# Attention and GEGLU on one core: the softmax sums of batches 3 to 6 move ahead of the next batch's scores, the products with v behind them

## The chip, the cores and the metric

The kernel runs on one core of a Trainium2 chip. Its time is the device time of one execution in microseconds (us); what is compared is the median of several executions. A profile is one execution recorded by the hardware. Engines: PE is TensorE (matmuls), DVE VectorE, ACT ScalarE, POOL GpSimd, SP SyncE (it only issues DMAs and semaphore work here). [...]

## The reference: what is computed

Windowed attention with a linear bias over 8 batches of 8 heads, 576 positions and head size 64, then a gated feed-forward block over all 8 x 576 = 4608 tokens:

```
scores = q @ k.T / 8 + slope[h] * -(i - j),  only for 0 <= i - j < 128
attn   = softmax(scores) @ v                       # per batch and head
x      = attn as [4608, 512]                       # 8 heads x 64 side by side
out    = (gelu(x @ w_gate) * (x @ w_val)) @ w_out  # 512 -> 1536 -> 512
```

All inputs and the output are float32; the kernel works in bfloat16 with float32 sums.

## The kernel before, in words

**Two pipelines on one TensorE.** Attention goes by batch (576 tokens), the feed-forward block by group g of 512 tokens, g = 0 to 8. A group has two parts. The *gate loop* is `gate_val(g, f)` for f = 0 to 11 (L608): eight matmuls of 128x512 each (L625, four with `wg` and four with `wv`, over the four 128-row slices c of `xT`), a gelu by ScalarE (L632), and a product by VectorE into the hidden tile `hT` (L633). The *steps* of the group, `steps(g)` (L906), write out the order of the rest by hand: an integer n stands for n sixteenths of the output product (`out_part`, L650; 4 is one quarter, 12 matmuls on L662, which ends with a copy of the bank to `osb` and a store on SP's queue), and names stand for attention work of batch b = g + 2.

**Attention of one batch.** q and k are loaded by POOL's queue (`load_qk`, L116), transposed by TensorE (`transposes`, L173, matmuls on L178) and copied to `qT`, `kT`. `scores2(b, c0)` (L260) makes the scores of four heads, half a batch: matmuls on L291 into six PSUM banks, six exponentials by ScalarE (L222), four masks by VectorE (L225), which leave the weights in `P`. Some of these matmuls share a bank between two halves of the array; for them `relay` (L201) puts an empty instruction on SP's queue, which waits for the first half's last matmul and lets the second half go. `add` (L371) is VectorE's preparation of the sums, into tile `T`. `sums4` (L419) makes the sums of the softmax with 32 small matmuls (L430) and inverts them with two VectorE reciprocals (L435) into a tile `r` that holds them in a compact form. To have them beside the products, they take a way through DRAM: `gather` (L439) writes them to `rd` in two small DMAs, `spread_dma` (L447) reads `rd` back twice, once for each half of the partitions, and copies each inverse to 64 partitions of tile `rb` (two DMAs of 576 KB). Both are on ACT's queue, and the spread waits for the gather to have landed. `values(b)` (L540) multiplies `P` with v (`products`, L457, matmuls on L494, six banks, with relays of the same kind) and scales the result by `rb` into `xT` (L558, VectorE: four slices of 512 columns, two small ones).

**Order around the change**, for the steps of g = 2 to 5 with b = g + 2: quarter 1; products of batch b - 1; quarter 2; scores of half 0 of batch b and their `add`; quarter 3; scores of half 1 and their `add`; quarter 4. In the gate loop of the next group follow: sums of the batch just scored at f 3 (f 4 in group 2), gather at f 5 (6), spread at f 7 (8), transposes of the batch after it at f 6 and 8, and at f 9 POOL's loads: q and k of batch g + 3 (ten DMAs), v of batch g + 2 (five). A one-element copy into `mark` holds POOL back until the hidden tile of that f is written.

**What the feed-forward block waits for.** Group g + 1 reads 512 tokens of `xT`, beginning at 512 (g + 1); for g + 1 up to 6 these include the first tokens of batch g + 1, which is batch b - 1 of the steps of group g. `xT` is a ring of 3072 tokens, so batch 5 is scaled in two pieces for each slice.

**Buffers.** The 8 PSUM banks are handed out in turn. `P`, `qT`, `kT`, q, k and v have two buffers (even and odd batches), `T`, `r` and `rb` one, `osb` three.

Of the kernel before, what the change touches and what calls it, by code (L numbers as in the profile page):

```python
# [8 lines left out]
BF16 = mybir.dt.bfloat16  # L9
# [23 lines left out]
def kernel(  # L33
# [10 lines left out]
    nc = tc.nc  # L44
    B, H, S, D = q.shape
# [22 lines left out]
    def bank():  # L68
        return psum.tile([128, 512], FP32, name="ps")
# [23 lines left out]
    mark = consts.tile([1, 2], BF16, name="mark")  # L93
# [22 lines left out]
    def load_qk(b):  # L116
        load(qs[b % 2], q, b)
        load(ks[b % 2], k, b)

    def load_v(b, js=range(5)):  # L120
        load(vb[b % 2], v, b, js, 64)
# [79 lines left out]
    def relay(mm, engine=nc.sync):  # L201
        by = engine.nop()
        depends(by, mm)
        return by
# [52 lines left out]

    def scores2(b, c0):  # L260
        pairs = (c0, c0 + 1)
        own, shared = {}, {}
        own[c0, 1] = bank()
        for c in pairs:
            shared[c] = bank()
        for key in ((c0, 0), (c0 + 1, 1), (c0 + 1, 0)):
            own[key] = bank()
        turns = ([(c, True) for c in pairs] + [(c, False) for c in pairs],
                 [(c, False) for c in pairs] + [(c, True) for c in pairs])
        todo, left = [], {}  # L270
        for i, turn in enumerate(turns):
            at = 0
            for c, both in turn:
                if both and i:
                    at = max(at, left[c] + HANDOVER)
                for x in (0, 1):
                    t = at
                    for m, q0, w, col in parts_of(x, both):
                        todo.append((t, i, c, both, x, m, q0, w, col))
                        t += w  # L280
                at = t
                left[c] = at
            if not i:
                left = {c: 256 * (n + 1) for n, c in enumerate(pairs)}
        todo.sort(key=lambda t: t[0])
        count, by = {c: 0 for c in pairs}, {}
        total = sum(len(parts_of(x, True)) for x in (0, 1))
        for _, i, c, both, x, m, q0, w, col in todo:
            half = slice(64 * i, 64 * i + 64)
            ps, col = (shared[c], col + 256 * i) if both else (own[c, i], col)  # L290
            mm = nc.tensor.matmul(  # L291
                out=ps[64 * x:64 * x + 64, col:col + w], lhsT=keys(b, c, m)[half, :],
                rhs=qT[b % 2][half, c, q0:q0 + w], start=True, stop=True)
            if both and i == 0:
                count[c] += 1
                if count[c] == total:
                    by[c] = relay(mm)
            if both and i and c in by:
                depends(mm, by.pop(c))

        def whole(c, i):
            exp(prob(b)[:, c, i, 64:576], own[c, i])

        def ends(c):
            exp(prob(b)[:, c, :, 576:832], shared[c][:, 0:512].rearrange("p (i x) -> p i x", i=2))

        def masks_(c, s):
            mask(prob(b)[:, c, :, 64 + 384 * s:448 + 384 * s], decay(s, c))

        c, d = pairs  # L310
        whole(c, 1)
        whole(c, 0)
        masks_(c, 0)
        ends(c)
        masks_(c, 1)
        ends(d)
        whole(d, 1)
        whole(d, 0)
        masks_(d, 0)
        masks_(d, 1)  # L320
# [50 lines left out]
    def add(b, c0, copy=None, what=(0, 1)):  # L371
        hs = slice(2 * c0, 2 * c0 + 4)
        P = Ps[b % 2].rearrange("p h (n y) -> p h n y", y=64)[:, hs]
        to = T.rearrange("p h (n y) -> p h n y", y=64)[:, hs]
        if 0 in what:
            for x in (0, 1):
                half = slice(64 * x, 64 * x + 64)
                nc.vector.tensor_tensor(  # L378
                    out=to[half, :, x:x + 7:2], in0=P[half, :, 0:10:3], in1=P[half, :, 1:11:3],
                    op=ALU.add)  # L380
            nc.vector.tensor_copy(out=to[0:64, :, 8], in_=P[0:64, :, 12])
            nc.vector.tensor_tensor(
                out=to[64:128, :, 8], in0=P[64:128, :, 11], in1=P[64:128, :, 12], op=ALU.add)
        if 1 in what:
            for x in (0, 1):
                half, n = slice(64 * x, 64 * x + 64), 4 - x
                (copy or nc.vector.tensor_copy)(
                    out=to[half, :, x + 1:x + 2 * n:2], in_=P[half, :, 2:3 * n:3])

    sumrow, recip = {}, {}  # L390
# [45 lines left out]

    flat = {}

    def gather(b):  # L439
        flat[b] = d_pool.tile([H, S], FP32, name="rd")  # L440
        for s in (0, 1):
            lo, w = shape(b, s)
            nc.scalar.dma_start(
                out=flat[b][:, lo:lo + 2 * w].rearrange("h (x t) -> x h t", x=2),
                in_=sumrow[b][0:128:8, lo:lo + w])

    def spread_dma(b):  # L447
        for i in (0, 1):
            nc.scalar.dma_start(
                out=recip[b][64 * i:64 * i + 64, :, :],  # L450
                in_=flat[b][i:H:2, :].unsqueeze(0).to_broadcast((64, 4, S)))

# [153 lines left out]
    hid = {}  # L606
# [34 lines left out]
    acc = {}  # L641


    by_dve = {0: (0,), 1: (0, 1)}

# [69 lines left out]
    for h in (0, 2, 4, 6):  # L717
        for w, src in ((0, q), (1, k)):
            (nc.scalar if w and h == 0 else nc.sync).dma_start(  # L719
                out=raw[w][h // 4].rearrange("p (h x) -> p h x", h=4)[:, h % 4:h % 4 + 2, :],  # L720
                in_=src[0][h:h + 2, 0:384, :].rearrange("h (p r) d -> p h (r d)", r=3))
# [115 lines left out]
    for do in inverse_a:  # L837
        do[1]()
    dve(out=pairs1.rearrange("p x (h d) -> p h x d", d=64),
        in_=vb[1].rearrange("p j x -> p (j x)")[:, 0:1536].rearrange(  # L840
            "p (h x d) -> p h x d", h=H, x=3))
# [46 lines left out]
    for n in range(4):  # L888
        nc.gpsimd.dma_start(
            out=wo[:, 3 * n:3 * n + 3, :],  # L890
            in_=moe_w_out[384 * n:384 * n + 384, :].rearrange("(c p) f -> p c f", p=128))
# [14 lines left out]
    def steps(g):  # L906
        b = g + 2
        if g in todo:
            return todo[g]
        if b > B:  # L910
            return [16] if g < NG - 1 else [12, ("last", g)]
        if b == B:
            return [4, ("pv", b - 1), 12]
        return [("table",), 4, ("pv", b - 1), 4, ("s2", b, 0), ("add", b, 0), 4, ("s2", b, 2),
                ("add", b, 2), 4]


    def exp_table():
        nc.scalar.preload_act_table_set("natural_log_exp_and_others")

    RUN = {"s": scores, "s2": scores2, "add": add, "sum4": sums4, "gather": gather, "spread": spread_dma, "pv": values, "pv+": values_and_sums,
           "masks": flush, "table": exp_table, "transposes": transposes, "last": out_last, "scale": lambda: scales.pop()(), "o": out_half}

    for g in range(NG):
        for f in range(9 if g == 0 else 0, NF):
            gate_val(g, f)
            if g == 1 and f in (5, 7):
                transposes(2, f - 5)
                transposes(2, f - 4)
            if g == 1 and f == 11:  # L930
                transposes(3, 0)
                transposes(3, 1)
                nc.gpsimd.tensor_copy(out=mark, in_=hid[g][0:1, f, 0:2])
                load_qk(4)
                load_v(3)
            if 2 <= g < B - 2 and f in (6, 8):
                transposes(g + 2, f - 6)
                transposes(g + 2, f - 5)
            if g == 2 and f == 2:
                add(3, 2, act, (1,))  # L940
            if g == 0 and f == 10:
                masks_of_last_blocks(0, 8)
            if g == 0 and f == 9:
                for c in range(4):
                    for w in (0, 1):
                        transpose(1, w, c, (act, dve)[w])
            if 2 <= g < B - 1:
                if f == (4 if g == 2 else 3):
                    sums4(g + 1)
                if f == (6 if g == 2 else 5):  # L950
                    gather(g + 1)
                if f == (8 if g == 2 else 7):
                    spread_dma(g + 1)
                if f == 9 and g + 2 < B:

                    nc.gpsimd.tensor_copy(out=mark, in_=hid[g][0:1, f, 0:2])  # L956
                    if g + 3 < B:
                        load_qk(g + 3)
                    load_v(g + 2)
        if g == 0:  # L960
            nc.gpsimd.memset(Ps[0][:, :, 0:64], 0.0)
        for item in steps(g):
            if isinstance(item, int):
                out_part(g, item)
            else:
                RUN[item[0]](*item[1:])
        store()
        if g == 0:
            load_qk(3)
            load_v(2)  # L970
# [30 lines left out]
```

## Time and profile before

| | |
|---|---|
| median of 3 executions | 361.46 us (360.63 to 361.49) |
| the profiled execution | 361.49 us; its span, first to last instruction, 359.7 us |
| granted TensorE clock | 1.000 |
| PE busy | 349.9 us (97% of the span) |
| DVE, ACT, POOL busy | 203.4, 184.4, 105.6 us |
| gate matmuls, L625 | 920, 52% of the chain that ended last |
| output matmuls, L662 | 24% of that chain |
| transposes L178, products L494, scores L291, sums L430 | 6%, 5%, 2%, 1% of that chain |
| one round of the steady part | 39.1 us (gate loop of group 3 from 182.61 to 207.74, its steps to 221.78) |

The chain that ended last is followed back from the last instruction: at each step to what released it, or to the instruction before it on its engine. Busy time of matmuls is modelled, since they overlap in the array; the durations in the chain are from start to start. Times in the timeline are microseconds from the start of the span.

### The profile page before, as it was taken

To read this page: it belongs to the slowest core of one execution; us is meant where nothing else is said; L and a number is where in the kernel's file an instruction comes from. 1 tells how busy PE (TensorE), PEld (TensorE's weight loads), DVE (VectorE), ACT (ScalarE), POOL (GpSimd) and SP (SyncE) were. 2 spreads that over 40 slices of the span, in tenths; PEclk is the share of its full clock that TensorE was granted. 3 is DMA by queue.
4 is the path that set the end of the run, shared out by engine and by line. 5 is a ranking of instruction groups with operands and counts; after the bars stand their busy time and mean duration, and the time that the engine had idled before them with its cause. 6 is when DMAs were issued, how large, how long until landed. Compare 5 with 4: busy or idle time off the path is not lost.

```text
span 359.7 us, 8537 instructions
## 1 busy us (share of the span) xinstructions
PE 349.9 (97%) x3508; PEld 184.7 (51%) x3556; DVE 203.4 (57%) x382; ACT 184.4 (51%) x340; POOL 105.6 (29%) x139
## 2 busy tenths in 40 slices
PE   8999999999999999999999999999999999999996
PEld 6667556555654555454545554455544544444444
DVE  7887865445789546944596458844694413302420
ACT  7964786447696437544473439253753123313322
POOL 6965689406700086004900192004000000000000
PEclk9999999999999999999999999999999999999999
DMA  8999999908950099219990599049203320011002
GB/s 210 171 197 191 200 187 187 124 2 52 162 107 2 5 194 189 64 23 135 170 122 5 131 138 181 3 104 105 81 31 69 95 89 2 0 58 60 0 28 90
DMA packets 118043, 35.65 MB, mean 99 GB/s; under 512 B 101716, under 2 KB 110964, under 8 KB 118004
## 3 DMA queue, kind: packets, MB, share of 16 engines
q0 software_dynamic: 107456, 18.10, 65.2%
q1 hardware_dynamic: 7232, 10.75, 8.5%
q10 hardware_dynamic: 3316, 6.25, 7.9%
q8 instruction: 28, 0.46, 0.5%
q14 instruction: 11, 0.09, 0.1%
HBM read 43.65 MB, written 9.53 MB: 148 GB/s over the span
## 4 chain that ended last, share of the span: by engine, by line
PE 94%; DMA 1%; issue 1%; DVE 1%; ACT 1%; SPq 0%; DVEq 0%
PE ps L625 52%; PE ps L662 24%; PE ps L178 6%; PE ps L494 5%; PE ps L291 2%; PE ps L682 2%; PE ps L209 1%; DMA qs<-in_q_dram 1%; PE ps L430 1%; PE ps L698 1%; PE ps L154 1%; ACT P L222 0%; SPq L719 0%; DVE xT L530 0%; DVE qT L162 0%
## 5 line engine op out<-in xcount | busy, mean ns | idle before, releaser
L633 DVE TENSOR_TENSOR hT<-ps,gelu 128x512 bf16<-128x512 f32 (+3 forms) x117 | 73.8, 646 | 97.6 <-PE ps L625 91.3
L632 ACT ACTIVATE gelu<-ps 128x512 bf16<-128x512 f32 (+3 forms) x117 | 65.1, 564 | 98.5 <-PE ps L625 96.2
L625 PE MATMUL ps<-xT,wg 128*128 128x512 bf16 (+4 forms) x460 | 112.1, 361 | 0.8
L625 PE MATMUL ps<-xT,wv 128*128 128x512 bf16 (+4 forms) x460 | 111.2, 361 | 0.4
L662 PE MATMUL ps<-wo,hT 128*128 128x512 bf16 x374 | 87.6, 380 | 2.1 <-issue 1.4
L625 PEld LDWEIGHTS <-wv 128*128 128x128 bf16 x472 | 45.0, 98 | 48.7
L625 PEld LDWEIGHTS <-wg 128*128 128x128 bf16 x472 | 43.5, 98 | 45.8
L662 PEld LDWEIGHTS <-hT 128*128 128x128 bf16 x396 | 37.0, 98 | 43.3
L222 ACT ACTIVATE P<-ps 128x512 bf16<-128x512 f32 (+1 forms) x108 | 51.3, 583 | 3.9 <-PE ps L209 3.6
L225 DVE TENSOR_TENSOR P<-P,emask 128x768 bf16<-128x768 bf16 x60 | 31.2, 556 | 19.5 <-ACT P L222 17.7
L667 ACT COPY osb<-ps 128x512 f32<-128x512 f32 x27 | 15.9, 588 | 51.3 <-PE ps L662 51.3
L112 POOL DMA_DIRECT2D vb<-in_v_dram x40 | 34.0, 902 | 2.9 <-DMA wo<-in_moe_w_out_dram 1.0
L956 POOL COPY mark<-hT 1x2 bf16<-1x2 bf16 x4 | 0.7, 174 | 108.4 <-DVE hT L633 108.4
L112 POOL DMA_DIRECT2D qs<-in_q_dram x30 | 25.5, 870 | 4.9 <-DMA wo<-in_moe_w_out_dram 2.7
L112 POOL DMA_DIRECT2D ks<-in_k_dram x30 | 25.4, 893 | 0.3 <-PE ps L625 0.3
L181 ACT COPY qT<-ps 128x576 bf16<-128x576 bf16 x22 | 14.0, 638 | 9.8 <-PE ps L178 9.8
L494 PE MATMUL ps<-P,vb 64*64 64x192 bf16 (+2 forms) x752 | 17.7, 221 | 0.6 <-issue 0.4
L558 DVE TENSOR_TENSOR xT<-ps,rb 128x512 bf16<-128x512 f32 (+3 forms) x34 | 14.7, 502 | 4.6 <-PE ps L494 4.6
L494 PEld LDWEIGHTS <-vb 64*64 64x64 bf16 x752 | 14.7, 107 | 4.0 <-issue 3.0
L181 DVE COPY kT<-ps 128x576 bf16<-128x576 bf16 x24 | 11.0, 457 | 5.7 <-PE ps L178 5.1
L378 DVE TENSOR_TENSOR T<-P 64x1024 bf16<-64x1024 bf16 x20 | 13.7, 686 | 0.6
L178 PE MATMUL ps<-ident,ks 128*128 128x128 bf16 (+1 forms) x120 | 12.7, 218 | 0.0
(95 smaller groups left out, 238.0 us busy)
## 6 DMA issues: line engine op xcount, KB each, us to landing
out_dram<-osb SPq DMA_DIRECT2D x35, 256.0 KB, 3.1
rb<-rd ACTq DMA_DIRECT2D x10, 576.0 KB, 6.4
vb<-in_v_dram POOLq DMA_DIRECT2D x32, 128.0 KB, 6.3
qs<-in_q_dram POOLq DMA_DIRECT2D x24, 128.0 KB, 4.5
ks<-in_k_dram POOLq DMA_DIRECT2D x24, 128.0 KB, 6.1
wo<-in_moe_w_out_dram POOLq DMA_DIRECT2D x4, 384.0 KB, 12.3
wg<-in_moe_w_gate_dram POOLq DMA_DIRECT2D x5, 256.0 KB, 8.4
wv<-in_moe_w_val_dram POOLq DMA_DIRECT2D x5, 256.0 KB, 8.9
```

The source lines that it names most:

```text
L112: nc.gpsimd.dma_start(out=t[at:at + n, j, :].rearrange("p (h d) -> p h d", h=H), in_=src[b][:, 128 * j:128 * j + n, :].rearrange("h p d -> ...
L178: nc.tensor.transpose(out=ps[:, 128 * j:128 * j + n], in_=src[b % 2][0:n, j, 128 * c:128 * c + 128], identity=ident[0:n, 0:n])
L181: copy(out=dst[b % 2][:, c, 0:S], in_=ps[:, 0:S])
L222: nc.scalar.activation(out=dst, in_=src, func=AF.Exp, scale=0.125)
L225: nc.vector.tensor_tensor(out=dst, in0=dst, in1=m, op=ALU.mult)
L494: mm = nc.tensor.matmul(out=out, lhsT=lhsT, rhs=prob(b)[half, c, i, col:col + q1 - q0], start=all(t[2] != u for t in todo[:n]), stop=True, ...
L558: nc.vector.tensor_tensor(out=xT[:, c, at:at + e - a], in0=src, in1=recip[b][:, c, a:e], op=ALU.mult)
L625: nc.tensor.matmul(out=ps[:, a:e], lhsT=w[:, c, 128 * f:128 * (f + 1)], rhs=xT[:, c, t0 + lo + a:t0 + lo + e], start=begins and a == 0, st ...
L632: nc.scalar.activation(out=gl[:, 0:n], in_=pg, func=AF.Gelu)
L633: nc.vector.tensor_tensor(out=hid[g][:, f, lo:hi], in0=pv, in1=gl[:, 0:n], op=ALU.mult)
L662: nc.tensor.matmul(out=acc[g], lhsT=hid[g][:, f, 128 * t:128 * (t + 1)], rhs=wo[:, f, :], start=(f == 0), stop=(f == NF - 1))
L667: (nc.vector.tensor_copy if g < B - 2 and t in by_dve.get(g, (0,)) else nc.scalar.copy)(out=osb, in_=acc[g])
```

## The change

Four things are changed together; the matmuls stay the same in number and shape.

- In the steps of groups 2 to 5 the order becomes: quarter 1; sums of batch b - 1; scores of half 0 of batch b; gather and spread of batch b - 1; quarter 2; scores of half 1; loads of v of batch b; quarter 3; products of batch b - 1; quarter 4. The `add` instructions of batch b go into the next gate loop, in four pieces at f 1, 2, 4 and 5.
- Gather and spread of batches 3 to 6 are on SP's queue instead of ACT's. The relays of half 1 are on POOL instead of SP.
- In groups 2 to 5 the copy of the first quarter goes from VectorE to ScalarE (`by_dve`).
- q and k of batch g + 3 are loaded from f 6 on instead of f 9. POOL starts the loads of v when the last inverse of partition 0 has landed in `rb`. Batch 7 keeps its sums in the gate loop of group 6, with the adds at f 0 to 3, the sums at f 5, the gather at f 7 and the spread at f 9.

The few words that came with the change also name transposes by TensorE in place of DMA transposes; the diff has no such lines, and the kernel before has those transposes on TensorE.

```diff
-    def scores2(b, c0):
+    def scores2(b, c0, engine=nc.sync):
...
-                    by[c] = relay(mm)
+                    by[c] = relay(mm, engine)
...
-    def gather(b):
+    def gather(b, queue=nc.scalar):
...
-            nc.scalar.dma_start(
+            queue.dma_start(
                 out=flat[b][:, lo:lo + 2 * w].rearrange("h (x t) -> x h t", x=2),
                 in_=sumrow[b][0:128:8, lo:lo + w])
 
-    def spread_dma(b):
+    def spread_dma(b, queue=nc.scalar):
         for i in (0, 1):
-            nc.scalar.dma_start(
+            queue.dma_start(
...
-    by_dve = {0: (0,), 1: (0, 1)}
+    by_dve = {0: (0,), 1: (0, 1), 2: (), 3: (), 4: (), 5: ()}
...
-        return [("table",), 4, ("pv", b - 1), 4, ("s2", b, 0), ("add", b, 0), 4, ("s2", b, 2),
-                ("add", b, 2), 4]
+        return [("table",), 4, ("sum4", b - 1), ("s2", b, 0), ("gather", b - 1, nc.sync),
+                ("spread", b - 1, nc.sync), 4, ("s2", b, 2, nc.gpsimd), ("load v", b), 4, ("pv", b - 1), 4]
+
+    def load_v_behind(b):
+        nc.gpsimd.tensor_copy(out=mark, in_=recip[b - 1][0:1, 0, S - 1:S].bitcast(BF16))
+        load_v(b)
...
-            if 2 <= g < B - 1:
-                if f == (4 if g == 2 else 3):
+            if 3 <= g < B - 1:
+                turns = (0, 1, 2, 3) if g == B - 2 else (1, 2, 4, 5)
+                if f in turns:
+                    n = turns.index(f)
+                    add(g + 1, n // 2 * 2, None, (n % 2,))
+            if g == B - 2:
+                if f == 5:
                     sums4(g + 1)
-                if f == (6 if g == 2 else 5):
+                if f == 7:
                     gather(g + 1)
-                if f == (8 if g == 2 else 7):
+                if f == 9:
                     spread_dma(g + 1)
-                if f == 9 and g + 2 < B:
-
-                    nc.gpsimd.tensor_copy(out=mark, in_=hid[g][0:1, f, 0:2])
-                    if g + 3 < B:
-                        load_qk(g + 3)
-                    load_v(g + 2)
+            if 2 <= g < B - 3 and f == 6:
+
+                nc.gpsimd.tensor_copy(out=mark, in_=hid[g][0:1, f, 0:2])
+                load_qk(g + 3)
```

More of the change, by code (lines that the diff above doesn't have):

```diff
@@ L913, in steps @@
             return [4, ("pv", b - 1), 12]
-        return [("table",), 4, ("pv", b - 1), 4, ("s2", b, 0), ("add", b, 0), 4, ("s2", b, 2),
-                ("add", b, 2), 4]
+        return [("table",), 4, ("sum4", b - 1), ("s2", b, 0), ("gather", b - 1, nc.sync),
[3 more added lines that the diff above has]
+        load_v(b)
     def exp_table():
         nc.scalar.preload_act_table_set("natural_log_exp_and_others")
-    RUN = {"s": scores, "s2": scores2, "add": add, "sum4": sums4, "gather": gather, "spread": spread_dma, "pv": values, "pv+": values_and_sums,
+    RUN = {"s": scores, "s2": scores2, "add": add, "sum4": sums4, "gather": gather, "spread": spread_dma, "pv": values, "load v": load_v_behind, "pv+": values_and_sums,
            "masks": flush, "table": exp_table, "transposes": transposes, "last": out_last, "scale": lambda: scales.pop()(), "o": out_half}
```

## The prediction

> **What bounds the kernel now.** I read the page first (shares by engine, and the chain that ended last), then the chain in order of time for one round of the steady part, then the timeline of the sums, the reciprocals and their two DMAs. The page:
>
> ```profile
> PE 349.9 (97%) x3508; PEld 184.7 (51%) x3556; DVE 203.4 (57%) x382; ACT 184.4 (51%) x340; POOL 105.6 (29%) x139
> ...
> PE 94%; DMA 1%; issue 1%; DVE 1%; ACT 1%; SPq 0%; DVEq 0%
> ```
>
> TensorE holds 94% of the chain. A reordering that leaves its matmuls as they are can only win small change-over costs, and it can lose wherever TensorE is made to wait. The chain from the steps of group 2 into the gate loop of group 3 (start, duration, what):
>
> ```profile
> 168.80 2.59 PE ps L662 x12
> 171.39 1.53 PE ps L494 x76
> 172.92 0.16 issue
> 173.07 2.54 PE ps L662 x11
> 175.61 0.80 PE ps L291 x32
> 176.41 0.32 PE ps L662
> ...
> 179.11 0.80 PE ps L291 x32
> ```
>
> The reader is to see a quarter of out products (L662), batch 3's products with v (L494), a second quarter, and the two halves of batch 4's scores (L291), each followed by another quarter of about 2.7 us; the gate loop follows at 182.61. No piece is a wait on another engine. Batch 4's sums come later, in the gate loop (same view):
>
> ```profile
> 189.51 0.61 PE ps L430 x32
> 190.13 0.32 PE ps L625
> ```
>
> The timeline of that stretch shows what hangs on these sums (start, duration, engine, line):
>
> ```profile
> 190.23 1.96 DVE L435 RECIPROCAL r<-ps 128x128 f32<-128x128 f32 x2
> ...
> 192.87 1.09 ACTq L443 DMA_DIRECT2D rd<-r  x2
> ...
> 198.30 1.30 ACTq L449 DMA_DIRECT2D rb<-rd  x2
> ```
>
> The second of the two spreads alone (the view of tile rb, cut to its issue):
>
> ```profile
> L449 ACTq DMA_DIRECT2D rb<-rd x1: 635/635/635, 199.0 to 199.0; - x1
> ...
> DMA to landing us min/median/max: 7.3/7.3/7.3
> ```
>
> So batch 4's inverses were on chip at 199.0 + 7.3 = 206.3, and their first user, the scaling after batch 4's products, began at 211.5, 5 us later: here this long way costs nothing. The scaling itself, from the groups by form in 172 to 176 us (busy, mean ns | idle before):
>
> ```profile
> L558 DVE TENSOR_TENSOR xT<-ps,rb 128x512 bf16<-128x512 f32 x4 | 2.5, 684 | 0.4 <-PE ps L494 0.4
> ```
>
> **What the change moves.** In the steps of groups 2 to 5 the sums of batch g+1 move from the gate loop to just behind the first quarter, and the products with v of the same batch move from behind the first quarter to behind the third. Sums, reciprocals, gather, spread, scaling and the next group's first matmul now all lie in one stretch. The next gate loop needs that scaling at once: group 3 reads tokens 1536 to 2047 and batch 3 begins at 1728, and likewise up to group 6 (tokens 3072 to 3583) with batch 6 (from 3456). Before, three quarters and two score halves (9.7 us) lay between products and gate loop; now one quarter does.
>
> **TensorE's cover**, from the start of the sums to the gate loop's first matmul: sums 0.61, scores 0.80, quarter 2.70, scores 0.80, quarter 2.70, products 1.53, quarter 2.70 (0.16 + 2.54): 11.84 us. The gate loop takes its four 128-row slices of xT in turn at 6.91 / 32 = 0.216 us each, so slice 3 is wanted at 11.84 + 0.65 = 12.49.
>
> **The chain beside it**, from the same start (189.51 in the trace):
> - Reciprocals begin 0.72 later and take 1.96: done at 2.68. VectorE is free for them; its last work of the gate loop, a 0.69 us product at 207.85, lies inside the first quarter.
> - The second gather is issued at about 2.75, from SP's queue now. Its issue is 0.53 us long; in the finest windows its packets ran from 194.5 to 194.9, up to 1.5 us after its issue began at 193.4. No landing is recorded. Lower bound 1.5 (the last packet); upper bound 3.1 (median of a 256 KB store). I take 2.2, the landing of the 128 KB store at the end, the nearest row of a small write to DRAM: 4.95.
> - The two spreads wait for it. First issue 0.64; the second lands 7.3 after its own issue (7.1 to 7.5 over the five pairs of the run, none with other traffic beside it): 4.95 + 0.05 + 0.64 + 7.3 = 12.95. The packets fill the 16 engines (share about 1.0 from 200 to 204.5), so another queue has nothing to speed up; SP could issue faster than ACT, by at most 0.6.
> - The scaling reads all 128 partitions and so needs both spreads: four slices in 2.5 us, the last done at 15.5. With a semaphore, 15.55.
>
> So slice 3 comes 15.55 - 12.49 = 3.06 us late: TensorE stops for about 1.2 us plus the first scaling, then creeps at VectorE's pace. I take **3.1 us a step, in four steps (groups 2 to 5): 12.4 us**. By the bounds (gather 1.5 to 3.1, spread 7.1 to 7.5) it is 2.2 to 4.2 a step.
>
> On the clock in such a stop: the granted clock is 1.00 in every microsecond from 0 to 22, though TensorE is busy only 0.45 of the one at 7, so I charge nothing. [...]
>
> **Won.** Sums in the gate loop force two changes of matmul shape: the matmul after them shows 0.32 instead of 0.216, and 0.05 of issue. Beside the scores one of these falls away: 0.1 a step, 0.4 in all; bounds 0 and 0.2 a step.
>
> **Costed at nothing, and the cover.**
> - Banks: eight in turn. The second half's scores take the sums' bank and five of the first half's. ScalarE empties six in 3.05 us, from about 1.2 to 4.2 after the start of the sums; the half begins at 4.1 and wants the fifth of them at most. The products begin at 7.6 and want five banks of the second half, emptied from 4.8 to 7.4. Without this slack a few tenths, which the stop behind them swallows, since the inverses set the end.
> - First quarters' copies to ScalarE (0.58 instead of VectorE's 0.69, four times): ScalarE had idled 6.00 us there.
> - Adds inside the gate loop (2.7 us of VectorE a half batch, in two pieces): VectorE idles about 1.0 us in each f of 1.73 us. Before, they delayed the first hT until 187.81 and TensorE never waited.
> - SP: the gather and the spread wait there with the first quarter's store, the second's and the products' relays behind them. The spread issues end near 6.3, two stores of 0.33 follow, the relays are due at 8.3. The fourth quarter's copy takes the first one's buffer (three in turn) and waits for its store, which is queued behind the spread; ScalarE may stand until about 14, still ahead of the first gelu.
> - The relays of the second half go to POOL, which has issued its ten loads by then. Uncovered: 0.2 to 0.3 a step, as SP's relay once cost the products (211.4).
> - q and k loads start at f 6 rather than 9: ten issues from 196.2 to 205.2 in the trace's time, and packets for some 4 us more (v loads issued from 244.9 to 249.1 kept engines busy until 253), to about 209.6. The spread is issued near 214.6.
> - v loads wait for the first spread and lie between it and the next f 6. Batch 7 has its sums at f 5; its scaling ends about 4 us before group 7 needs it.
> - Transposes: the words of the change speak of them, but the diff leaves them alone (L178 is on TensorE already). They give nothing.
>
> **Sum.** The profiled execution took 361.49 (span 359.7), 0.03 from the median of 361.46. 361.49 + 12.4 - 0.4 = **373.5**.
>
> **Rivals.**
> 1. The chain fits under the cover: not slower. It decides at the landing of the second spread: 12.49 - 2.5 = 10.0 after the start of the sums instead of 12.95, so gather and spread together would need 3 us less. Then only the 0.4 stays: 361.1, at best 360.7. For it: a faster issue on SP. Against it: 5.6 us of packets at full share. 0.05.
> 2. A smaller stop, 0.5 to 2.2 us a step, if both DMA legs land earlier than their rows: 361.49 - 0.4 + 2 to 8.8, so 363 to 370. For it: I have no landing of the gather. Against it: five like spreads. 0.07.
> 3. The spread meets the q and k loads. While those run, the engines' share stands near 2 at 110 to 150 GB/s. If the spread gets half the engines, its 5.6 us double in the three steps with such loads (groups 2 to 4): + 16.8, 390. It needs loads that last 5 us longer than worked out. 0.04.
> 4. The change does nothing of weight, because the products' place was never tight in either order: 361. The 5 us of slack before speak for it, the arithmetic above against it. 0.03.
>
> Forecast 0.81. The range, 368 to 379, takes in the bounds of the two legs (361.49 + 8.8 - 0.8 = 369.5 to 361.49 + 16.8 = 378.3) and part of rival 2. About 0.3% (1.1 us) is what a measurement of this kernel can tell from no change. Rival 4 and 0.03 of rival 1 lie within it; the other 0.02 of rival 1 is for relays and banks that give a little as well (below 360.4). Faster 0.02, same 0.06, slower 0.92.
>
> **What would show it.** After: in each of four steps, idle time on TensorE before the gate line L625 of f 0, released by the scaling (L558), itself idle until DMA rb; the chain leaving TensorE there for DVE and DMA, 3 us each; nothing of the kind before groups 7 and 8. Reciprocals end 2.7 us after the sums begin, the second spread lands about 13 after. I am wrong if the rb landing comes before 10, or if TensorE waits elsewhere, for a bank or a relay.

## The result, and the profile after

The changed kernel takes 378.03 us (median of 4, 376.40 to 378.83) against 361.04 (median of 4): 1.0466 times as long, 95% interval 1.0426 to 1.0507. Its profiled execution took 377.76 us with a span of 376.0. Forecast were 373.5, in a range of 368 to 379.

From the page after, TensorE's busy time, the granted clock in 40 slices, and the chain by engine:

```profile
PE 357.5 (95%) x3508; PEld 186.1 (49%) x3556; DVE 200.6 (53%) x378; ACT 187.7 (50%) x344; POOL 106.2 (28%) x142
...
PEclk9999999999999998999999998999989999999999
...
PE 80%; DMA 11%; DVE 5%; issue 1%; SPq 1%; ACT 1%; DVEq 0%
```

Two things are new. TensorE holds 80% of the chain instead of 94%, and DMAs 11%, VectorE 5%. And the clock line, all 9 before, has three slices with an 8. The chain in order of time through the steps of group 3 (start, duration, what), windowed to 168 to 200:

```profile
174.90 0.64 PE ps L430 x32
...
175.56 1.98 DVE r L435 x2
...
177.56 1.74 DMA rd<-r
...
179.43 0.62 SPq L449
...
180.09 7.33 DMA rb<-rd
...
187.54 2.50 DVE xT L558 x4
...
190.08 7.93 PE ps L625 x36
198.01 0.05 issue
```

The reader is to see that between the sums and the gate loop the path leaves TensorE: reciprocals, gather, spread, scaling, each beginning as the one before ends. TensorE's list of waits (total, times, longest) has one entry of weight, where before no entry came above 1.4 in total:

```profile
PE ps L625 <- DVE xT L558: 9.1, 15, 2.2
```

The clock, in windows cut at its changes (window, length, PE busy, PEld, DVE, ACT, POOL, then granted clock, DMA share, GB/s):

```profile
142.99:146.41 3.42, 0.82 (x3) 0.21 (x3) 1.93 (x4) 1.38 (x2) 3.42 (x5) 1.00 1.49 278
146.41:149.82 3.41, 3.39 (x8) 1.09 (x8) 1.32 (x4) 1.08 (x2) 0.20 (x1) 0.50 1.97 187
187.37:190.78 3.41, 1.85 (x7) 0.65 (x8) 2.88 (x6) 2.16 (x3) 2.27 (x3) 1.00 1.91 226
190.78:194.19 3.41, 3.41 (x18) 1.52 (x17) 1.73 (x3) 1.15 (x3) 0.00 (x0) 1.00 1.41 150
```

After the stop of group 2's steps the clock stands at 0.50 for 3.41 us, in which TensorE starts 8 matmuls, by its timeline, where group 4's gate loop (190.78) starts 16 at full clock. (The x8 and x18 of the rows count all that are under way at some time in the window.) The same happens at 231.74 and 276.11; the stop of group 3 is not followed by it.

So the bill of the four steps, all from the chain in order of time (sums begin; slice 3 of the gate loop begins; late against 12.49; the 37 matmuls from there, 7.99 at 0.216 each). The chain names 36 and then 0.05 of issue: the timeline has three of the four matmuls of one product there in the time of four, so one has no record, and the column runs to the start of the matmul behind it (198.06 in group 3).

| steps of group | sums | slice 3 | after | late | 37 matmuls | over 7.99 |
|---|---|---|---|---|---|---|
| 2 | 131.19 | 147.01 | 15.82 | 3.33 | 9.36 | 1.37 |
| 3 | 174.90 | 190.08 | 15.18 | 2.69 | 7.98 | -0.01 |
| 4 | 216.59 | 231.76 | 15.17 | 2.68 | 9.65 | 1.66 |
| 5 | 259.94 | 275.48 | 15.54 | 3.05 | 9.67 | 1.68 |

That is 11.75 of waiting and 4.70 of slow matmuls, 16.45 in all; the two profiled executions differ by 377.76 - 361.49 = 16.27, so 0.2 is won elsewhere, 0.05 a step.

### The profile page after: what moved, and what is told of

The parts are those of the page before. It is cut to its first block, busy times and chain, and to the rows that moved or that the text cites. A ratio compares the mean times of both kernels' runs of the same rounds, so it can differ in the third digit from the quotient of the medians.

```text
span 376.0 us, 8536 instructions
## 1 busy us (share of the span) xinstructions
PE 357.5 (95%) x3508; PEld 186.1 (49%) x3556; DVE 200.6 (53%) x378; ACT 187.7 (50%) x344; POOL 106.2 (28%) x142
## 3 DMA queue, kind: packets, MB, share of 16 engines
q1 hardware_dynamic: 9552, 15.54, 13.8%
## 4 chain that ended last, share of the span: by engine, by line
PE 80%; DMA 11%; DVE 5%; issue 1%; SPq 1%; ACT 1%; DVEq 0%
PE ps L625 51%; PE ps L662 14%; DMA rb<-rd 8%; PE ps L178 6%; PE ps L494 3%; DVE xT L558 2%; DVE r L435 2%; DMA rd<-r 2%; PE ps L209 1%; PE ps L682 1%; DMA wo<-in_q_dram 1%; PE ps L430 1%; SPq L449 1%; PE ps L698 1%; PE ps L154 1%
## 5 line engine op out<-in xcount | busy, mean ns | idle before, releaser
L633 DVE TENSOR_TENSOR hT<-ps,gelu 128x512 bf16<-128x512 f32 (+3 forms) x117 | 75.0, 648 | 103.4 <-PE ps L625 98.3
L625 PE MATMUL ps<-xT,wg 128*128 128x512 bf16 (+4 forms) x463 | 116.7, 367 | 9.8 <-DVE xT L558 9.1
L625 PE MATMUL ps<-xT,wv 128*128 128x512 bf16 (+4 forms) x460 | 113.9, 368 | 0.4
L667 ACT COPY osb<-ps 128x512 f32<-128x512 f32 x31 | 18.2, 587 | 55.1 <-PE ps L662 31.1
L435 DVE RECIPROCAL r<-ps 128x128 f32<-128x128 f32 (+1 forms) x10 | 9.8, 1026 | 9.8 <-PE ps L430 9.8
```

Of the source, the lines that this page charges most:

```text
L435: nc.vector.reciprocal(row(b)[:, first:first + w], ps[:, at:at + w])
L625: nc.tensor.matmul(out=ps[:, a:e], lhsT=w[:, c, 128 * f:128 * (f + 1)], rhs=xT[:, c, t0 + lo + a:t0 + lo + e], start=begins and a == 0, st ...
L633: nc.vector.tensor_tensor(out=hid[g][:, f, lo:hi], in0=pv, in1=gl[:, 0:n], op=ALU.mult)
L667: (nc.vector.tensor_copy if g < B - 2 and t in by_dve.get(g, (0,)) else nc.scalar.copy)(out=osb, in_=acc[g])
```

## The experiments

The theory: the loss is the wait for the inverses, whose way from the sums has a fixed length, plus what the clock loses after a stop. Rival A: the new order costs by itself, by relays, SP's queue, banks or ScalarE's copies. Rival B: the slow stretches come from the v loads that run beside them. Each run stands against runs of the kernel before on the same chip (361.0 to 361.1 in all).

**Without the way through DRAM.** Batches 3 to 6 are scaled by batch 2's inverses; gather and spread of these batches are left out.

```diff
...
+        recip[b - 1] = recip[2]
-        ... ("s2", b, 0), ("gather", b - 1, nc.sync), ("spread", b - 1, nc.sync), 4, ...
+        ... ("s2", b, 0), 4, ...
```

> The changed kernel without the way through DRAM for batches 3 to 6: gather and spread are left out there, and the products of these batches are scaled by the inverses of batch 2, so that part of the result is not computed. Sums and reciprocals stay. Theory (the stop is the wait for the inverses, and the half clock follows from the stop): no stop before any gate loop, granted clock 1.000, 360 to 361.5 us. Rival A (the new order itself costs: relays on POOL, SP's queue, banks, copies on ScalarE): still above 370.

Measured: 360.91 us, ratio 0.9991 (0.9978 to 1.0004), clock 1.0. The chain through the steps of group 3, which is the cover that the prediction added up to 11.84:

```profile
169.49 0.61 PE ps L431 x32
170.10 0.80 PE ps L291 x32
170.90 2.70 PE ps L663 x12
173.60 0.81 PE ps L291 x30
174.41 2.70 PE ps L663 x12
177.11 1.53 PE ps L495 x76
178.64 2.70 PE ps L663 x12
181.33 12.09 PE ps L626 x56
```

Not a tenth is lost from the sums to the gate loop (181.33 - 169.49 = 11.84), with relays on POOL, copies on ScalarE and the late products all in place. Rival A is out, but for SP's queue, which this run also relieves of gather and spread; the run with half the bytes, below, keeps them there and loses nothing either. So what the change costs hangs on the inverses. From one batch's products to the next it is 38.85 us, against 38.93 to 39.17 before: 0.1 to 0.3 a round, the saving at the sums. The ratio's interval reaches to 1, so as a gain in time it isn't shown.

**TensorE kept busy in the stop.**

```diff
+    def busy(n):
+        keep_busy(bank(), n, 512, wo[:, 0, :])
...
-        ... ("load v", b), 4, ("pv", b - 1), 4]
+        ... ("load v", b), 4, ("pv", b - 1), 4, ("busy", 8)]
```

> The changed kernel with eight idle matmuls of 512 columns (on zeros) between the last quarter and the gate loop of groups 3 to 6, on a bank of their own. Theory (the clock falls because TensorE stands for 2 us and then creeps): the inverses land as late as before, about 12.5 after the sums begin, but the clock stays at 1.000, and the 5.3 us of the three slow stretches go: 372 to 373. Rival B (the slow stretches come from the loads of v, which run at the same time with the DMA engines' share above 2): clock and time stay, 377 to 379.

Measured: 372.96 us, ratio 1.0324 (1.0303 to 1.0345), clock 1.0. The chain in the steps of group 3:

```profile
174.26 0.64 PE ps L430 x32
...
179.46 7.75 DMA rb<-rd
...
187.33 2.50 DVE xT L558 x4
...
189.86 5.34 PE ps L625 x24
```

Slice 3 comes 15.6 after the sums, no earlier than in the changed kernel, and the 24 recorded matmuls from there take 5.34 (0.22 each). The v loads run as before (the DMA engines move 236 and 239 GB/s from 140 to 150 and from 183 to 193 us, against 235 and 239 in the changed kernel), so rival B is out: more matmuls make the kernel 5.1 us faster, and the clock stays up (1.000 in the profiled execution, 0.985 in the changed kernel's). The rest, 372.96 - 361.02 = 11.9, is the wait itself.

**Gather and spread on ACT's queue, relays on SP**, as before the change.

```diff
-("s2", b, 0), ("gather", b - 1, nc.sync), ("spread", b - 1, nc.sync), 4, ("s2", b, 2, nc.gpsimd), ...
+("s2", b, 0), ("gather", b - 1), ("spread", b - 1), 4, ("s2", b, 2), ...
```

> The changed kernel with gather and spread on ACT's queue and the relays on SP, as before the change. Theory: ScalarE reaches the gather only behind six exponentials, about 4.3 after the sums begin instead of 2.7, and stands at the spread until the gather has landed, so that copies and exponentials behind it are late too. Inverses about 2 us later a step, products held up by their banks as well: 386 or more. Rival A (SP's queue and POOL's relays are what costs): less than 378.

Measured: 372.77 us, ratio 1.0313 (1.0284 to 1.0342), clock 1.0 in three of four executions, 0.995 in the other. Below 378, as rival A had it, but not for its reason. The timeline of ScalarE, with its queue:

```profile
175.40 1.08 ACT L222 ACTIVATE P<-ps 128x512 bf16<-128x512 f32 x2 [0.40 <-PE ps L291]
176.03 0.53 ACTq L443 DMA_DIRECT2D rd<-r  x1
176.37 1.09 ACT L222 ACTIVATE P<-ps 128x512 bf16<-128x512 f32 x2
177.05 0.53 ACTq L443 DMA_DIRECT2D rd<-r  x1
```

The gather is issued between the exponentials, not behind all six: ScalarE's queue handed out DMAs while earlier activations were still to start, four of six at 176.03 and two at 177.05. My expectation was wrong there: it took ScalarE's DMAs and activations to go strictly in the order of the program. The second gather goes out 2.67 after the sums began (174.38), the scaling begins at 187.15, 12.77 after them (12.64 in the changed kernel), slice 3 at 189.69, 15.3 after: the same chain on another queue. What differs is where TensorE stands. Its waits:

```profile
PE ps L625 <- DVE xT L558: 4.9, 15, 1.1
PE ps L494 <- ACT P L222: 1.6, 8, 0.2
```

ScalarE's work behind the spread is late, so the products wait 0.2 us at a time for the exponentials that empty their banks, and the last stop in the steps of group 3 is 0.6 instead of 1.1 us. The standing is spread out, the clock does not fall in the profiled execution, and the time is that of the run with idle matmuls. That the spreading is what saves the clock is argued here, from the count of windows further down; no run tried it alone.

**Sums, gather and spread back in the gate loop**, the products still late.

```diff
-("sum4", b - 1), ("s2", b, 0), ("gather", b - 1, nc.sync), ("spread", b - 1, nc.sync), 4, ...
+("s2", b, 0), 4, ...
...
+            if 2 <= g < B - 2 and f == 6:
+                sums4(g + 1)
+                gather(g + 1, nc.sync)
+                spread_dma(g + 1, nc.sync)
```

> The changed kernel with one part undone: sums, gather and spread of batches 3 to 6 go back into the gate loop, at f 6 behind the adds; the products stay behind the third quarter, the DMAs stay on SP, the relays on POOL, the first quarter's copy on ScalarE. Theory: the inverses are on chip long before; the scaling takes 2.5 us under a quarter of 2.7, so no stop: 361 to 362, clock 1.000. Rival C (the products are too late by themselves, with the scaling behind eight masks on VectorE): a stop of 0.5 us or more a step remains, 363 to 366.

Measured: 360.98 us, ratio 0.9997 (0.9984 to 1.0011), clock 1.0, and no wait of TensorE for VectorE's scaling. Putting the products behind the third quarter costs nothing as long as the inverses are there; rival C is out. It is the sums that were moved to the wrong place for that.

**Sums ahead of the first quarter**, which lengthens the cover by 2.6.

```diff
-[("table",), 4, ("sum4", b - 1), ("s2", b, 0), ("gather", b - 1, nc.sync), ("spread", b - 1, nc.sync), 4, ...
+[("table",), ("sum4", b - 1), ("gather", b - 1, nc.sync), ("spread", b - 1, nc.sync), 4, ("s2", b, 0), 4, ...
```

> The changed kernel with sums, gather and spread one quarter earlier, ahead of the first quarter of the steps; all else as changed. Theory (a chain of fixed length against the cover of TensorE): the last slice of xT still comes 15.2 us after the sums begin, but is now wanted 2.6 us later, at 15.1: a stop of at most 0.3 us a step, clock 1.000, 361 to 362. Rival A (something else in the new order stops TensorE): 365 or more.

Measured: 373.5 us, ratio 1.0344 (1.0323 to 1.0364), clock 0.991. Far off, and by the number rival A's. The timeline shows the fault:

```profile
175.50 1.31 SPq L449 DMA_DIRECT2D rb<-rd  x2
...
176.92 0.42 PE L291 MATMUL ps<-qT,kT 64*64 64x64 bf16 x12 [1.95 <-SPq L202]
```

The edit put the first half's scores behind gather and spread, and their relays are on SP. SP waited there for the gather to land, issued the spread, and only then came to the relays: TensorE stood 1.9 us a step, 7.7 in all, and the clock fell twice. In the changed kernel the first half's relays come before the gather, and the second half's are on POOL, so this didn't happen there. Mended:

```diff
-... 4, ("s2", b, 0), 4, ("s2", b, 2, nc.gpsimd), ...
+... 4, ("s2", b, 0, nc.gpsimd), 4, ("s2", b, 2, nc.gpsimd), ...
```

> The kernel with sums, gather and spread ahead of the first quarter, with one line more: the relays of the first half of the scores go to POOL as well as those of the second. In the run without it these relays stood on SP behind gather and spread, and TensorE waited for them 1.9 us a step. Theory (chain against cover, and that wait was a fault of the experiment's order alone): TensorE's wait for SP goes; the last slice of xT comes 15.2 to 15.6 us after the sums begin and is wanted at 15.1: a stop of at most 0.5 us a step, clock 1.000, 361 to 363. Rival A (something else in the new order stops TensorE): 365 or more.

Measured: 362.69 us, ratio 1.0042 (1.0026 to 1.0059), clock 1.0. TensorE's waits:

```profile
PE ps L625 <- DVE xT L558: 0.9, 4, 0.2
```

In the steps of group 3 slice 3 begins 15.98 after the sums (167.38 to 183.36), against 12.49 + 2.6 = 15.1: the chain is still 0.9 too long there, mostly because the second spread takes 8.09 us instead of 7.33 (7.67 and 7.81 in the steps of groups 4 and 5). 2.6 us more of cover bring 378.0 to 362.7; with the whole of the gate loop from f 6 on as cover it was 361.0.

**Half the bytes.**

```diff
+            if b in (3, 4, 5, 6):
+                sumrow[b] = sumrow[b].bitcast(BF16)[:, 0:S]
+                recip[b] = recip[b].rearrange("p c x -> p (c x)").bitcast(BF16)[:, 0:4 * S].rearrange(
+                    "p (c x) -> p c x", c=4)
...
-        flat[b] = d_pool.tile([H, S], FP32, name="rd")
+        flat[b] = d_pool.tile([H, S], BF16 if b in (3, 4, 5, 6) else FP32, name="rdh" if b in (3, 4, 5, 6) else "rd")
```

> The changed kernel with the inverses of batches 3 to 6 in bfloat16 from the reciprocals on (tiles r, rd and rb), so that gather and spread move half the bytes in as many packets. Theory, if bytes set the spread's 5.6 us: the spread lands 2.8 us earlier, the last slice is there at 12.4 where it is wanted at 12.5: a stop of at most 0.3 us a step, clock 1.000, 360.5 to 362. Rival D (the number of packets sets it, 32 for each engine): landing as late as before, 376 to 379.

Measured: 361.29 us, ratio 1.0003 (0.9990 to 1.0016), clock 1.0. The two spreads of group 3's steps:

```profile
L454 SPq DMA_DIRECT2D rb<-rdh x2: 617/617/617, 173.9 to 174.6; - x2
...
DMA to landing us min/median/max: 3.6/3.9/4.2
```

The same two in the changed kernel:

```profile
DMA to landing us min/median/max: 5.4/6.3/7.3
```

Half the bytes, 288 instead of 576 KB in each, bring the second landing from 7.3 to 4.2 us: here bytes set the spread's time (rival D is out). With 3 us less VectorE's scaling still waits for it in three steps, by 0.8 us at most, but TensorE no longer waits for the scaling:

```profile
DVE xT L563 <- DMA rb<-rdh: 2.3, 3, 0.8
```

In the order of the changed kernel this alone takes the loss away.

**Fewer idle matmuls**, to see when the clock falls: `("busy", 3)` instead of 8.

> The changed kernel with three idle matmuls of 512 columns (0.65 us) instead of eight ahead of the gate loops. In the changed kernel the clock fell at ends of a grid of 3.413 us whose last window was busy for about 19, 20 and 37 per cent, and did not fall where it was 41. Theory (a window on that grid that is busy for less than some 40 per cent halves the clock): 0.65 us lifts the windows to 38 to 60 per cent, so at most one fall of four: 372.5 to 375, clock 0.995 or more. Rival E (an unbroken stand of a microsecond or more is enough, wherever it lies): stands of 0.5 to 1.5 us remain, two or three falls, 376 to 378.

Measured: 375.24 us, ratio 1.0370 (1.0335 to 1.0405). The profiled execution had two falls, ahead of its end, where I expected one at most:

```profile
PEclk9999999999999999999989999999989999999999
```

The four executions sort by mean clock: 372.69 us at 0.999, 374.80 at 0.995, 376.04 at 0.991, 375.68 at 0.990. Two falls cost (375.86 - 372.69) = 3.2, 1.6 each, with a single execution without a fall to set them against. The expectation's 40 per cent held in the steps of groups 2 to 5 (falls behind windows of 34 and 32%, none behind 58%, in the table below), my guess of how much 0.65 us would fill did not. I laid windows of 3.413 us, the length of a fall in the changed kernel, end to end so that one ends where a fall begins, and took for each the time of the matmuls started in it (0.216 us for 512 columns, those side by side in the array once) as a share. The two kernels without a fall there have their windows from the first and last record of the clock. The expectation's 19, 20, 37 and 41 were a first count; this one gives:

| kernel | windows followed by a fall | lowest windows without a fall, steps of groups 2 to 5 |
|---|---|---|
| changed | 13, 19, 37% | 40% |
| three idle matmuls | 34, 32% | 58% |
| sums ahead of the first quarter | 36, 35% | 52, 59% |
| ACT's queue | none | 50, 52, 54, 57% |
| eight idle matmuls | none | 60% |

So, by this count, falls followed windows of up to 37% busy and none followed a window of 40% or more. The stop of group 3, which no fall followed, was split over two windows: TensorE stood from 187.14 to 188.29, and one window ends at 187.37. Rival E, a stand of a microsecond as such, doesn't fit: the changed kernel stood 1.14 us in group 3's steps without a fall, and with three idle matmuls falls followed two stops and not the other two.

**The best of it together**: half the bytes, the products' relays on POOL, v loads behind the products, batch 7's sums one f later.

```diff
-... ("s2", b, 2, nc.gpsimd), ("load v", b), 4, ("pv", b - 1), 4]
+... ("s2", b, 2, nc.gpsimd), 4, ("pv", b - 1), ("load v", b), 4]
...
-relay(mm, nc.vector if b in (1, 2) else nc.sync)
+relay(mm, nc.vector if b in (1, 2) else nc.gpsimd if b in (3, 4, 5, 6) else nc.sync)
...
-                if f == 5:
+                if f == 6:
                     sums4(g + 1)
-                if f == 7:
+                if f == 8:
                     gather(g + 1)
-                if f == 9:
+                if f == 10:
```

> The changed kernel with the inverses of batches 3 to 6 in bfloat16, the relays of these batches' products on POOL with the loads of v behind them, and batch 7's sums one f later (f 6, gather f 8, spread f 10), where they no longer wait for its adds. Theory: no stop; a round is 0.2 us shorter than before the change by the sums beside the scores, 0.3 and 0.4 us go with the waits at batch 7's sums and at one products' relay: 360 to 361, at best 0.3% under the kernel before. Rival F (these are too small, or POOL's relay is slower than SP's): 361 to 362, within its scatter.

Measured: 360.89 us, ratio 1.0001 (0.9987 to 1.0015), clock 1.0. The waits named are gone from TensorE's list, but the kernel is not shown to be faster than the one before. Where TensorE has 94% of the chain, what these edits can give is below the scatter of the runs.

## Why the prediction was right, and where it was not

- *The sign and the mechanism* were right: sums, reciprocals, gather, spread and scaling in one stretch, longer than TensorE's work beside it. Without the DRAM way the loss is gone; with half its bytes too.
- *Cover 11.84*: measured 11.84.
- *Chain*: reciprocals done 2.64 after the sums began (2.68 predicted); gather landed 1.74 after its issue (2.2 taken, 1.5 to 3.1 as bounds); second spread 7.3 after its issue (7.3) and 12.5 after the sums (12.95; its terms add up to 12.94); scaling done at 15.1 (15.5). These are group 3's steps. In those of groups 2, 4 and 5 the second spread took 8.0, 7.5 and 7.7, twice above the 7.5 taken as upper bound; why is open.
- *3.1 a step, 12.4 in all*: measured 2.68 to 3.33, together 11.75, and 11.9 by the run with the clock held up, which has the small gain in it.
- *Won 0.4*: 0.2 by the bill, between the bounds of 0 and 0.8; the ratio of the run without the wait doesn't tell it from nothing.
- *The clock, "so I charge nothing"*: this step failed. The row I argued from, one microsecond at 0.45 busy, lies in 3.41 us that are 52% busy by the count above (5.04 to 8.45). The 3.41 us ahead of the changed kernel's falls were 13, 19 and 37% busy, so the row shows nothing about a stop with a creep behind it. Nor is the 1.00 up to 5.04 us a measurement: the record of the clock begins there, and the views print 1.00 where there is none. The falls cost 5.1 us by the busy run (378.03 - 372.96), 4.7 by the bill. 373.5 + 5.1 = 378.6 would have been the sum. That 378.03 lies inside the range is owed in part to its upper bound, which had been set by the two DMA legs and had no room of its own for the clock.
- *Costs put at nothing* stayed nothing: no wait of TensorE for a bank above 0.2; ScalarE stood for the first quarter's store until 13.1 after the sums, ahead of the first gelu; the products waited 0.2 once for a relay on SP. The run with the relays behind the spread shows what that one would cost out of place: 1.9 a step.
- *Rival 3*, the meeting with q and k loads, did not come: in the microsecond before each of the four spreads the DMA engines' share was 0.04 or less.

On the clock, the rows: in the changed kernel each of the three falls ahead of its end lasts 3.413 us at 0.50, and they begin whole multiples of that apart (146.41 to 231.74 is 25 of them, 231.74 to 276.11 is 13). From these rows 3.413 * 0.50 = 1.7 us would be the estimate for a fall; measured are 1.6 by the runs with three idle matmuls and 1.4 to 1.7 by the bill. The stretch of that length ahead of a fall was never quite idle, and one 37% busy was still followed by a fall.

## What to carry to other kernels

Before a producer is moved next to its consumer, add up everything between them, DMA landings from the trace included, and set it against the work that the bottleneck engine still has in between; an engine-side time that looked free was free only because of the distance. Three of the four stops here cost 1.4 to 1.7 us beyond their length, in the 3.41 us at 0.50 behind them. So where a stop can't be removed, try idle matmuls in it; here eight in each stop saved 5.1 us. The same waiting in small pieces, as in the run on ACT's queue, went with as much (378.03 - 372.77 = 5.3). And look for relays behind a DMA that waits for a landing: on SP's queue, behind the spread, they held TensorE up for 1.9 us a step.

## What the runs showed of the hardware that was not expected

- In the changed kernel the granted clock went to 0.50 at 146.41, 231.74 and 276.11, for 3.413 us each time; by the count above the same length ahead of these was 13, 19 and 37% busy. In the steps of the five kernels of the table falls followed windows of 13 to 37%, and none followed one of 40% or more. The 38% from 3.05 to 6.46 us of the changed kernel, without a fall, lie ahead of the clock's record, where TensorE was slow already: 128-column matmuls start 0.107 us apart before the record begins (6.46 us) and 0.056 after. From there on 40% is the lowest window without a fall in that kernel, and 52% in the kernel before.
- With gather and spread on ACT's queue, ScalarE's queue issued DMAs at 176.03 and 177.05 while four and two of six earlier exponentials were still to start.
- With 288 instead of 576 KB in each, two broadcasts in flight landed 3.6 and 4.2 us after their issues, instead of 5.4 and 7.3.
